# A fused attention and gated-layer kernel: first loads split over two queues, first projections k by k, and early copies shared by two engines

## Chip, cores and metric

One core of a Trainium2 chip. The metric is the device time of one execution in microseconds (us), median of several. A profile of one execution gives its span (first to last recorded instruction), what every engine did in it, and what each instruction waited for. PE is the tensor engine, PEld its weight loads, DVE the vector engine, ACT the scalar engine, POOL the general-purpose engine, SP the engine that issues most transfers.

## The reference, cut

```python
x = A_x                                   # [1, 2048, 512] bf16
xn = _layernorm(x, axis=-1)
# A: 32 heads of 16, causal, window of 256, then wo [512, 512]
#    q, k, v = xn @ wqkv [512, 1536];  p = softmax(mask(q k / 4));  o = p v;  A = o @ wo
# B: h = (xn @ w_gate) * (xn @ w_up)      [2048, 1792];  B = h @ w_down
return x + A + B
```

## The kernel before

The kernel has no fixed loop order. A planner in the kernel's source walks through the work with estimated durations and landing times and emits each instruction where its estimate says it will be ready. The tokens are taken in four chunks of 512; chunk 0 is projected in four blocks of 128 rows, since nothing else can run yet. Only these parts matter here:

```python
MM = 0.2158                       # the planner's unit of PE time
PSUM_COPY = {"V": (0.605, 0.69), "A": (0.49, 0.60)}   # took, latency on DVE / ACT
HOLD = 0.1
...
# prologue: the loads, in this order
load(nc.sync, self.Wqkv[:, 0:2, 1024:1536], w["qkv"][:, 0:2, 1024:1536])    # Wv, 256 KB
load(nc.scalar, self.x[:, 0, :], xv[:, 0, :])                               # x0, 128 KB
load(nc.sync, self.Wqkv[:, 2:4, 1024:1536], w["qkv"][:, 2:4, 1024:1536])    # Wv, 256 KB
load(nc.scalar, self.x[:, 1, :], xv[:, 1, :])                               # x1, 128 KB
for t, lo in ((2, 512), (3, 0)):                                            # Wk, x2, Wq, x3
    load(nc.sync, self.Wqkv[:, :, lo:lo + 512], w["qkv"][:, :, lo:lo + 512])
    load(nc.sync, self.x[:, t, :], xv[:, t, :])
...
self.keep_busy(42, 0)             # filler matmuls until the first real one
...
# planner: which engine takes a copy, and when a transpose may go first
key = (at + (0.3 if e == "A" and len(o.on) > 1 else 0.0) + (self.HOLD if o.rank and now0 else 0.0), o.rank, t)
t -= 0.3 * (d.name.startswith("turn") and t <= now + 0.25)
...
def first_chunk(self):
    land = (3.4, 3.95, 7.7, 9.6)  # planned landings of x0 to x3
    wv, wk, wq = 5.9, 7.3, 9.3    # and of the weights
    ...                           # per block b: bn_stats, bn_aggr (DVE), sqrt (ACT),
                                  # reciprocal, apply (DVE), transpose (PE, "turn"), copy of it, then V, K, Q
    last = self.op("masks", {"V": (0.15, 0.2)}, [self.at_["ap", 1, 0]], ...)
    def project(i, lo, tok=tok):
        for c in range(4):
            self.matmuls(self.M[i][:, 128 * c:128 * c + 128],
                         [(self.Wqkv[:, k, lo + 128 * c:lo + 128 * c + 128], self.xnT[0][:, k, tok]) for k in range(4)])
```

The softmax here doesn't subtract the row's maximum and nothing guards it: scores larger than these inputs give would overflow.

## Time and profile before

| | before |
|---|---|
| time, median of 3 (lowest to highest) | 265.63 us (265.57 to 265.79) |
| span of the profiled execution | 263.98 us |
| first transpose of real data on PE | 5.53 us |
| first gate matmul (steady work begins) | 15.50 us |
| last matmul starts | 260.22 us |
| last matmul to the end of the span | 3.75 us |

The rows below the span cut the execution into a start, a middle (from the first gate matmul to the last matmul, 244.72 us) and a tail. The pieces are compared by start times of single matmuls, because modelled ends hide gaps of up to 0.2 us. The lines of the page, of the waits, of the stretches and of the chain are in the prediction. One more view, the timeline of DVE (start, duration, engine, line, operation, tiles; in brackets the idle time ahead and what ended it):

```profile
3.41 0.69 DVE L591 BATCH_NORM_STATS2 st<-x 128x6 f32<-128x512 bf16 x1 [1.47 <-DMA x<-in_A_x_dram]
...
4.60 0.43 DVE L591 BATCH_NORM_STATS2 st<-x 128x6 f32<-128x256 bf16 x1 [0.29 <-DMA x<-in_A_x_dram]
```

The first line is the statistics of x0, as soon as it landed; the second is the first half of x1's, which waits 0.29 us for its load and holds x0's reciprocal behind it.

### The profile page before, as it was taken

To read this page: it belongs to the slowest core of one execution; us is meant where nothing else is said; L and a number is where in the kernel's file an instruction comes from. 1 tells how busy PE (TensorE), PEld (TensorE's weight loads), DVE (VectorE), ACT (ScalarE), POOL (GpSimd) and SP (SyncE) were. 2 spreads that over 40 slices of the span, in tenths; PEclk is the share of its full clock that TensorE was granted. 3 is DMA by queue.
4 is the path that set the end of the run, shared out by engine and by line. 5 is a ranking of instruction groups with operands and counts; after the bars stand their busy time and mean duration, and the time that the engine had idled before them with its cause. 6 is when DMAs were issued, how large, how long until landed. Compare 5 with 4: busy or idle time off the path is not lost.

```text
span 264.0 us, 8009 instructions
## 1 busy us (share of the span) xinstructions
PE 259.4 (98%) x3456; PEld 131.9 (50%) x3456; DVE 190.6 (72%) x368; ACT 165.0 (63%) x122; POOL 119.7 (45%) x272
## 2 busy tenths in 40 slices
PE   8999999999999999999999999999999999999994
PEld 7974444554444354455534354546535353545462
DVE  4999886978996548777997467786946268786504
ACT  3457576768776766687776767677777676572000
POOL 1406655475175635427084736437081828255000
PEclk9999999999999999999999999999999999999999
DMA  6999910000002200000005200000000100000002
GB/s 219 381 374 350 215 22 1 2 0 2 4 2 59 64 22 22 0 2 2 2 0 83 62 22 0 4 2 0 2 2 22 40 4 22 2 0 2 0 2 81
DMA packets 17251, 13.88 MB, mean 53 GB/s; under 512 B 7104, under 2 KB 17216, under 8 KB 17216
## 3 DMA queue, kind: packets, MB, share of 16 engines
q1 hardware_dynamic: 16784, 13.05, 18.0%
q8 instruction: 27, 0.44, 0.7%
q10 hardware_dynamic: 432, 0.33, 0.4%
q14 instruction: 8, 0.07, 0.1%
HBM read 9.70 MB, written 2.10 MB: 45 GB/s over the span
## 4 chain that ended last, share of the span: by engine, by line
PE 96%; DMA 2%; DVE 1%; ACTq 0%; issue 0%
PE M L207 72%; PE S L215 9%; PE M L245 7%; PE M L689 6%; DMA x<-in_A_x_dram 1%; DMA out_dram<-xn 1%; PE M L624 1%; PE S L207 1%; DVE xn L783 1%; DVE st L591 0%; ACTq L149 0%; DVE xn L273 0%; PE M L197 0%; DVE rs L603 0%
## 5 line engine op out<-in xcount | busy, mean ns | idle before, releaser
L498 ACT ACTIVATE P<-S 128x2048 bf16<-128x2048 f32 x76 | 140.9, 1854 | 57.1 <-PE S L215 50.5
L224 POOL TENSOR_SCALAR_AFFINE_SELECT P<-P 64x256 bf16<-64x256 bf16 (+1 forms) x248 | 112.6, 456 | 112.9 <-ACT P L498 100.7
L207 PE MATMUL M<-xnT,Wg 128*128 128x512 bf16 x224 | 57.7, 380 | 0.0
L207 PE MATMUL M<-xnT,Wu 128*128 128x512 bf16 x224 | 57.7, 380 | 0.0
L207 PE MATMUL M<-Wd,hT 128*128 128x512 bf16 (+1 forms) x224 | 51.8, 373 | 0.0
L741 DVE TENSOR_TENSOR hT<-M,gsb 128x512 bf16<-128x512 f32 x56 | 38.0, 678 | 8.4 <-PE M L207 8.1
L207 PEld LDWEIGHTS <-hT 128*128 128x128 bf16 x238 | 21.7, 98 | 23.4 <-issue 2.1
L207 PEld LDWEIGHTS <-Wu 128*128 128x128 bf16 x224 | 20.5, 98 | 24.8 <-issue 1.8
L207 PEld LDWEIGHTS <-Wg 128*128 128x128 bf16 x224 | 20.2, 98 | 24.3 <-issue 2.4
L203 DVE CAST gsb<-M 128x512 bf16<-128x512 f32 x41 | 28.1, 686 | 5.3 <-PE M L207 4.9
L207 PE MATMUL M<-xnT,Wqkv 128*128 128x128 bf16 (+1 forms) x224 | 30.3, 288 | 0.0
L215 PE MATMUL S<-Q,K 32*128 32x320 bf16 (+3 forms) x720 | 30.0, 254 | 0.0
L534 DVE STREAM_TRANSPOSE at<-M 128x512 f32<-128x512 f32 x32 | 21.3, 698 | 9.7 <-PE M L245 9.6
L215 PEld LDWEIGHTS <-K 32*128 32x128 bf16 x720 | 11.9, 92 | 31.8 <-issue 30.9
L230 DVE TENSOR_TENSOR P<-P,masks 128x512 int16<-128x512 int16 x56 | 22.6, 410 | 7.1 <-ACT P L498 7.1
L207 PEld LDWEIGHTS <-Wqkv 128*128 128x128 bf16 x224 | 15.9, 98 | 10.6 <-issue 1.5
L783 DVE TENSOR_TENSOR y<-M,x 128x512 bf16<-128x512 f32 x12 | 8.2, 687 | 16.5 <-PE M L207 16.3
L245 PE MATMUL M<-P,V 64*17 64x320 bf16 (+4 forms) x1440 | 19.5, 252 | 0.0
L245 PEld LDWEIGHTS <-V 64*17 64x17 bf16 x1440 | 17.1, 86 | 3.2 <-issue 1.3
L284 DVE TENSOR_SCALAR K<-M,own 128x512 bf16<-128x512 f32 x24 | 17.1, 743 | 2.1 <-PE M L207 2.1
L207 PE MATMUL M<-Wo,OT 128*128 128x512 bf16 (+1 forms) x64 | 16.6, 374 | 0.0
L689 PE MATMUL M<-Wqkv,xnT 128*64 128x256 bf16 x256 | 15.5, 274 | 0.0
(51 smaller groups left out, 138.0 us busy)
## 6 DMA issues: line engine op xcount, KB each, us to landing
Wg<-in_B_w_gate_dram SPq DMA_DIRECT2D x2, 896.0 KB, 10.2
Wu<-in_B_w_up_dram SPq DMA_DIRECT2D x2, 896.0 KB, 11.9
out_dram<-y SPq DMA_DIRECT2D x12, 128.0 KB, 1.7
Wqkv<-in_A_wqkv_dram SPq DMA_DIRECT2D x2, 512.0 KB, 6.1
x<-in_A_x_dram SPq DMA_DIRECT2D x1, 1024.0 KB, 13.6
Wd<-in_B_w_down_dram SPq DMA_DIRECT2D x2, 512.0 KB, 11.6
Wd<-in_B_w_down_dram SPq DMA_DIRECT2D x2, 384.0 KB, 8.7
Wqkv<-in_A_wqkv_dram SPq DMA_DIRECT2D x2, 256.0 KB, 3.5
```

What stands on the lines that cost most here:

```text
L203: self.nc.vector.tensor_copy(out=out, in_=in_)
L207: self.nc.tensor.matmul(ps, lhsT=a, rhs=b, start=first and n == 0, stop=last and n == len(pairs) - 1)
L215: self.nc.tensor.matmul(self.S[:, e, 64 * at:64 * (at + m)], lhsT=self.K[U % 3][rows, c, j].rearrange("p l t -> p (l t)"), rhs=self.Q[T % ...
L224: self.nc.gpsimd.affine_select(out=v, in_=v, pattern=[[0, 4], [0, n], [sign, 64]], base=0, fill=0.0, compare_op=ALU.is_gt if kind else ALU ...
L230: self.nc.vector.tensor_tensor(out=v, in0=v, in1=m, op=ALU.bitwise_and)
L245: self.nc.tensor.matmul(banks[lane][32 * e:32 * e + 17, 64 * q:64 * (q + m)], lhsT=self.V[U % 3][rows, j, 4 * c + e, 0:17], rhs=P[rows, e, ...
L284: self.nc.vector.tensor_scalar(out=out, in0=in_, scalar1=own, scalar2=None, op0=ALU.mult)
L498: ex = self.op(f"exp{g}", {"A": (took + 0.06, took + 0.18)}, [o], lambda e: self.nc.scalar.activation(out=P[:, :, 0:hi], in_=self.S[:, :, ...
L534: t = self.op(f"tr{v}", {"V": (0.63, 0.71)}, [o] + ts, lambda e, par=par: nc.vector.transpose(out=self.at[:, :, par, :], in_=self.M[banks[ ...
L689: self.nc.tensor.matmul(self.M[i][64 * lane:64 * lane + 64, 256 * jj:256 * jj + 256], lhsT=self.xnT[T % 2][:, k, tok], rhs=w[:, lane], sta ...
L741: x = self.op(f"u{T}.{f}", {"V": PSUM_COPY["V"]}, [o, ("gate", T, f)], lambda e: self.nc.vector.tensor_tensor(out=self.hT[T % 2][:, f, :], ...
L783: self.nc.vector.tensor_tensor(out=keep["y"][:, cols], in0=self.M[i][:, cols], in1=self.x[:, t, cols], op=ALU.add)
```

## The change

The intent: bring x1 early enough that DVE does not wait for it, bring Wv and Wk in pieces over both issuing queues, let a projection begin with the k pieces that are there (k numbers the four slices of 128 rows of a weight, which are summed up), spread the first chunk's copies over ACT and DVE alike, and build the masks when nothing needs DVE. The planner's estimates are renewed to match.

```diff
+KEYS_COPY = {"V": (0.68, 0.76), "A": (0.63, 0.70)}
-    HOLD = 0.1
+    HOLD = 0.2
@@ prologue
-        load(nc.sync, self.Wqkv[:, 0:2, 1024:1536], w["qkv"][:, 0:2, 1024:1536])
+        qkv(nc.sync, 1024, 0, 1)
         load(nc.scalar, self.x[:, 0, :], xv[:, 0, :])
-        load(nc.sync, self.Wqkv[:, 2:4, 1024:1536], w["qkv"][:, 2:4, 1024:1536])
-        load(nc.scalar, self.x[:, 1, :], xv[:, 1, :])
-        for t, lo in ((2, 512), (3, 0)):
-            load(nc.sync, self.Wqkv[:, :, lo:lo + 512], w["qkv"][:, :, lo:lo + 512])
-            load(nc.sync, self.x[:, t, :], xv[:, t, :])
+        load(nc.sync, self.x[:, 1, :], xv[:, 1, :])
+        qkv(nc.scalar, 1024, 2, 4)
+        qkv(nc.sync, 1024, 1, 2)
+        qkv(nc.scalar, 512, 2, 4)
+        qkv(nc.sync, 512, 0, 2)
+        load(nc.sync, self.x[:, 2, :], xv[:, 2, :])
+        qkv(nc.sync, 0, 0, 4)
+        load(nc.sync, self.x[:, 3, :], xv[:, 3, :])
-        for f, g in ((0, 4), (4, 8), (8, 11), (11, 14)):
+        for f, g in ((0, 7), (7, 14)):
             load(nc.sync, self.Wd[:, f:g], w["d"][:, f:g])
@@ run, loop, choose
-        self.now, self.mode = 5.4, "D"
-        self.free = {"V": 3.0, "A": 4.5, "G": 3.0, "S": 6.0}
+        self.now, self.mode = 4.8, "D"
+        self.free = {"V": 3.0, "A": 3.4, "G": 3.0, "S": 6.0}
-  key = (at + (0.3 if e == "A" and len(o.on) > 1 else 0.0) + ...
+  key = (at + (0.3 if e == "A" and len(o.on) > 1 and not now0 else 0.0) + ...
-  t -= 0.3 * (d.name.startswith("turn") and t <= now + 0.25)
+  t -= 0.5 * (d.name.startswith("turn") and t <= now + 0.4)
@@ first_chunk
-        land = (3.4, 3.95, 7.7, 9.6)
-        wv, wk, wq = 5.9, 7.3, 9.3
+        land = (3.45, 3.9, 7.2, 9.6)
+        wv, wk, wq = 5.4, 6.6, 9.2
-        last = self.op("masks", {"V": (0.15, 0.2)}, [self.at_["ap", 1, 0]], ...
+        last = self.op("masks", {"V": (0.15, 0.2)}, [self.at_["ap", 3, 0]], ...
-                for c in range(4):
-                    self.matmuls(self.M[i][:, 128 * c:128 * c + 128],
-                                 [(self.Wqkv[:, k, lo + 128 * c:lo + 128 * c + 128], self.xnT[0][:, k, tok]) for k in range(4)])
+                for k in range(4):
+                    for c in range(4):
+                        self.nc.tensor.matmul(
+                            self.M[i][:, 128 * c:128 * c + 128], lhsT=self.Wqkv[:, k, lo + 128 * c:lo + 128 * c + 128],
+                            rhs=self.xnT[0][:, k, tok], start=k + c == 0, stop=k == 3, skip_group_check=True)
  ... (copies of K planned with KEYS_COPY; transposes, V, K and Q of chunk 0 planned shorter) ...
```

More of the change, by code (lines that the diff above doesn't have):

```diff
@@ L149, in load, with qkv @@
             eng.dma_start(out=dst, in_=src)
-        load(nc.sync, self.Wqkv[:, 0:2, 1024:1536], w["qkv"][:, 0:2, 1024:1536])
+        def qkv(eng, lo, k0, k1):
+            load(eng, self.Wqkv[:, k0:k1, lo:lo + 512], w["qkv"][:, k0:k1, lo:lo + 512])
+        qkv(nc.sync, 1024, 0, 1)
         load(nc.scalar, self.x[:, 0, :], xv[:, 0, :])
-        load(nc.sync, self.Wqkv[:, 2:4, 1024:1536], w["qkv"][:, 2:4, 1024:1536])
-        load(nc.scalar, self.x[:, 1, :], xv[:, 1, :])
-        for t, lo in ((2, 512), (3, 0)):
-            load(nc.sync, self.Wqkv[:, :, lo:lo + 512], w["qkv"][:, :, lo:lo + 512])
-            load(nc.sync, self.x[:, t, :], xv[:, t, :])
+        load(nc.sync, self.x[:, 1, :], xv[:, 1, :])
[6 more added lines that the diff above has]
+        load(nc.sync, self.x[:, 3, :], xv[:, 3, :])
         h = self.F // 2
@@ L338, in loop @@
                     at = max(t, self.free[e])
-                    key = (at + (0.3 if e == "A" and len(o.on) > 1 else 0.0) + (self.HOLD if o.rank and now0 else 0.0), o.rank, t)
+                    key = (at + (0.3 if e == "A" and len(o.on) > 1 and not now0 else 0.0) + (self.HOLD if o.rank and now0 else 0.0), o.rank, t)
                     if best is None or key < best[0]:
@@ L611, in first_chunk @@
             out=self.warm[:], in_=self.warm[:], func=ACT.Exp), rank=1)
-        last = self.op("masks", {"V": (0.15, 0.2)}, [self.at_["ap", 1, 0]], lambda e: nc.vector.memset(self.masks[:], -1), rank=9)
+        last = self.op("masks", {"V": (0.15, 0.2)}, [self.at_["ap", 3, 0]], lambda e: nc.vector.memset(self.masks[:], -1), rank=9)
         for n in range(5):
@@ L643, in k_out @@
                 for lane in range(2):
-                    x = self.op(f"K0b{b}", PSUM_COPY, [o, x], lambda e, lane=lane: self.i_keys(
+                    x = self.op(f"K0b{b}", KEYS_COPY, [o, x], lambda e, lane=lane: self.i_keys(
                         e, 0, slice(0, 4), lane, self.M[i].rearrange("p (c t) -> p c t", c=4), slice(2 * b, 2 * b + 2)), rank=1)
@@ L658, in first_chunk @@
             for n, ks in enumerate(([0, 1], [2, 3]) if b == 0 else ([0, 1, 2, 3],)):
-                self.A.insert(at + n, Dense(f"turn{b}", 1.3 * len(ks) / 4, [("ap", b, n)], lambda i, f=turn, ks=ks: f(i, ks),
+                self.A.insert(at + n, Dense(f"turn{b}", 1.1 * len(ks) / 4, [("ap", b, n)], lambda i, f=turn, ks=ks: f(i, ks),
                                             lambda o, i, f=turned, ks=ks: f(o, i, ks)))
             self.add_v(0, b, wv)
-            self.add(f"k0b{b}", 4.85, [("xnT", 0, b), wk], lambda i, f=project: f(i, 512), k_out)
-            self.add(f"q0b{b}", 4.85, [("xnT", 0, b), wq], lambda i, f=project: f(i, 0), q_out)
+            self.add(f"k0b{b}", 4.4, [("xnT", 0, b), wk], lambda i, f=project: f(i, 512), k_out)
+            self.add(f"q0b{b}", 4.4, [("xnT", 0, b), wq], lambda i, f=project: f(i, 0), q_out)
     def norms(self, T):
@@ L699, in add_v @@
         x = [("xnT", T, b)] if T + b else [("xnT", 0, 0, 0), ("begun", 0, 0, 2)]
-        self.add(f"v{T}.{b}", 4 if T else 4.4, x + [land] + self.ring(T, 2)[:1 if T == 3 else 0], emit, evac, "C")
+        self.add(f"v{T}.{b}", 4, x + [land] + self.ring(T, 2)[:1 if T == 3 else 0], emit, evac, "C")
     def add_qk(self, T, c):
@@ L708, in k_out @@
             for lane in range(2):
-                x = self.op(f"K{T}.{c}", PSUM_COPY, [o, x], lambda e, lane=lane: self.i_keys(
+                x = self.op(f"K{T}.{c}", KEYS_COPY, [o, x], lambda e, lane=lane: self.i_keys(
                     e, T, slice(c, c + 1), lane, self.M[i].unsqueeze(1)), rank=1)
```

## The prediction

> **What bounds the kernel now.** I read the page first (busy shares), then the waits of PE, then the stretch table, then the chain of waits and the timeline of the first 16 us. One core, so no dies to compare; its granted clock is 1.00.
>
> ```profile
> span 264.0 us, 8009 instructions
> PE 259.4 (98%) x3456; PEld 131.9 (50%) x3456; DVE 190.6 (72%) x368; ACT 165.0 (63%) x122; POOL 119.7 (45%) x272
> ```
>
> PE is the only engine near its limit. Its waits over the whole span, as the trace attributes them, are two:
>
> ```profile
> PE M L197 <- PEq L817: 0.8, 1, 0.8
> PE M L624 <- DVE xn L273: 0.2, 1, 0.2
> ```
>
> The first is the launch, the second the wait for the first normalised rows. The stretch table (columns: us, then busy us and count of PE, PEld, DVE, ACT, POOL, clock, DMA share, GB/s) confirms it:
>
> ```profile
> 5.50:10.50 5.00, 4.92 (x76) 4.20 (x76) 4.43 (x14) 1.60 (x5) 2.31 (x10) 1.00 1.04 364
> 10.50:15.50 5.00, 4.97 (x89) 4.92 (x89) 4.87 (x12) 4.15 (x8) 0.70 (x3) 1.00 1.07 374
> 20.50:240.00 219.50, 219.50 (x2985) 103.73 (x2982) 165.15 (x310) 155.02 (x105) 113.51 (x248) 1.00 0.13 30
> 240.00:264.00 24.00, 20.50 (x203) 11.27 (x201) 9.06 (x15) 0.00 (x0) 1.32 (x3) 1.00 0.07 24
> ```
>
> The reader is to see that from 5.5 us on PE has no visible idle time until about 260.5 us; after that come 3.5 us of last additions and stores. The change touches the loads, the first chunk and the costs by which the kernel's own planner orders work. So only the time before steady work, and the little that PE loses between 5.5 and 17 us, is there to win. The chain of waits from the start of the span (start, us, what) shows the first part:
>
> ```profile
> 1.25 3.33 DMA x<-in_A_x_dram
> ...
> 4.60 0.43 DVE st L591
> 5.03 0.07 DVE rs L603
> 5.10 0.03 issue
> 5.13 0.36 DVE xn L273
> 5.49 0.05 issue
> 5.53 0.54 PE M L624 x4
> 6.08 0.23 PE M L197 x4
> 6.31 1.05 PE M L689 x16
> 7.36 0.04 issue
> 7.40 0.40 PE M L624 x4
> 7.79 2.75 PE M L207 x48
> 10.55 0.03 issue
> 10.58 0.40 PE M L624 x4
> ```
>
> The first real matmul (the transpose, L624) stands behind the load of x1, not of x0. x0's statistics end at 4.32 and its square root (ACT, 4.35 for 0.29) at 4.64. But DVE's program puts half of x1's statistics before x0's reciprocal. That half waits idle from 4.32 to 4.60 for x1, which landed at 4.58. So reciprocal and apply start about 0.28 us late, and so does the transpose. The filler matmuls (L197) end by then:
>
> ```profile
> 0.84 4.47 PE L197 MATMUL M<-const-bfloat16-1.0 128*128 128x128 bf16 x42 [0.84 <-PEq L817]
> 5.53 0.54 PE L624 MATMUL M<-ident,xn 128*128 128x128 bf16 x4 [0.22 <-DVE xn L273]
> ```
>
> PE's busy time hides more. A matmul's modelled end lies some 0.2 us after its last issue, so I also took start-to-start times of single matmuls. The hidden gaps after 5.1 us are 0.38 (filler to transpose), 0.14 (between the halves of the first transpose), 0.15 (filler to the V projection), 0.21 (V projection to the second transpose) and 0.19 (before the third transpose, whose input ends at 10.11 + 0.41 = 10.52): 1.07 us in all. Nothing else in the first chunk exceeds 0.1. The rest, about 16 us over 174 places, is some 0.1 us at each change between kinds of matmul (score, value, dense), spread over the whole run.
>
> **What the Trainium skill says.**
> - "TensorE: Matmul & The Clock Gate", section "Wait — 56ns, not 53.3ns?": warm matmuls of 128 columns follow each other at 55.6 ns. The trace agrees: 48 projections take 2.75 us in the chain, 57 ns each. So the projections already run at the pipeline's pace.
> - "DMA: Bandwidth & Descriptors", section "Issuing engines are not separate DMA queues": transfers from SP and ACT share the same 16 engines; another issuer saves only issue time. The trace has 0.43 to 0.50 us per issue on SP and 350 to 381 GB/s in the loaded slices. Two queues cannot load faster; they can only change what lands first.
> - "PSUM — Partial Sum Buffer", section "The four PSUM rules": the start flag clears the written-bits of a whole bank, so four interleaved sums in one bank need it on the first matmul only. The new loop does exactly this (start only at k = c = 0), so I expect right results; no run here shows it yet.
> - "ScalarE: Activation LUTs", section "What ACT_TABLE_LOAD costs": about 1283 ns per table load. The trace has 1.28 us, twice (1.74 and 13.64). The number of switches stays.
>
> **The change, part by part.**
>
> 1. Loads. Before x2, the same 256 KB of x, 512 KB of Wv and 512 KB of Wk are moved in both kernels. x1 goes from second on ACT, beside two 256 KB pieces of Wv, to second on SP behind one 128 KB piece. Between 4.02 and 5.11 us x1 and the second Wv piece (384 KB) landed, 357 GB/s. With x0 and the first piece landed near 3.4, x1 and an equal share of ACT's Wv piece are 256 KB, so 0.73 us: x1 at about 4.1 (estimate), before DVE asks at 4.32. DVE's idle 0.28 us goes, and the transpose can start at 5.53 - 0.28 = 5.25; the 42 fillers, unchanged, were last issued at 5.10. Gain 0.25. ACT issues one more load (0.45 us), so its first table load ends near 3.5 and its warm-up by 3.7, before the first root at 4.35: free.
>
> 2. Wk in halves on both queues. It landed at 7.54; the plan now counts on 6.6. The bytes ahead are the same. If it comes before the V projection ends (about 6.85), K of the first rows can fill the 0.21 us gap; otherwise the second transpose comes first, as now. The planner also allows a longer wait for a transpose (preference 0.5 instead of 0.3), so the gap may simply remain. I book 0.05 to 0.1.
>
> 3. k by k. The same 8 x 16 matmuls at 57 ns: no saving in work. 4.4 instead of 4.85 is only the planner's estimate (in units of 0.2158 us, 0.95 instead of 1.05; measured 0.91). The order lets a projection start with the pieces that are there, but Wv and Wk are needed late enough. Zero.
>
> 4. Copies on ACT and DVE alike until the first scores. In 10.5 to 15.5 DVE is busy 4.87 of 5 us; ACT has 4.15, but only 1.60 in the five before and an idle stretch of 2.64 us just before the first exp at 17.77. Moving copies to ACT takes load from DVE. PE had dense work in the meantime, so the gain is what PE waited: the 0.19 before the third transpose, of which I book 0.15. The first scores may move from 17.33 to about 16.5, but that pays nothing by itself: the same PE work follows, and exp has slack (ACT is 63% busy and does nothing after 240).
>
> 5. Masks later. One memset of 0.33 us leaves DVE at 7.35, where it delays a copy of V and a transposed copy. POOL's ten selects (2.86 us) start near 12.5 instead of 7.75 and end near 15.5, long before the first select at 19.72. PE was fed, so about 0.05, inside the item above.
>
> 6. Wd in two loads, not four: SP's issues are blocked there anyway and the data are needed much later. Zero.
>
> Sum: 0.25 + 0.1 + 0.15 + about 0.1 from the small gaps around the first transpose = 0.6 us. 265.63 - 0.6 = 265.0.
>
> **The rivals.**
> - Lost in replanning. New cost figures shift the first scores and with them the static order of about 76 score batches and 16 value groups. One score batch more or fewer that stands alone between dense work costs or saves two changes, about 0.19 us (6.7 us over 70 entries and 5.3 over 58 exits). Three either way is 0.55 us, as large as the gain. For: the plan is sensitive. Against: PE had no wait at all after 24 us, so the order had slack. It gives 264.5 to 265.6.
> - A load takes the place of the wait. Wv in three pieces on two queues could land later than the V projection asks, or the smaller pieces make x0 later than 3.39. For: Wk took 2.4 us after Wv for 512 KB, slower than the rest. Against: Wv had landed at 5.11 and is asked for at 6.05. If x0 slips 0.2 and Wk is late, 265.4 to 265.9.
> - ACT becomes the slow link. With no handicap, copies queue there in front of the roots that gate the transposes, and in front of the 1.28 us table load, so scores come later. For: an ACT copy takes 0.60 to 0.63 us. Against: ACT is idle for most of the first 10 us, and roots outrank copies. 265.3 to 266.
> - Everything works: all 1.07 us of gaps go, 264.5, and with a lucky replanning 264.2.
>
> **Range and chances.** The gain is bounded above by about 1.1 us of early gaps plus about 0.5 of planning luck, and a loss by a few waits of some tenths. Predicted 265.0, range 264.2 to 265.8. Two per cent is 5.3 us, five times the gaps available: faster 0.01, within 2% 0.98, slower 0.01.
>
> **What would show it.** Step 1: x1 landing before 4.32, no DVE idle before the second statistics, the first transpose at 5.25 to 5.35. Steps 2 and 4: gaps before the second and third transposes under 0.1, Wk landed before 7, K and V copies in ACT's rows before 13 us. Step 3: 48 projections still at 57 ns. Replanning: PE without waits after 24 us, and the number of changes of kind near 174. It would be wrong if PE shows a wait over 0.5 us after 6 us, if x1 still lands after 4.5, or if the last matmul moves by more than the first one did: then the middle, not the start, decided.

## The result, and the profile after

| | before | after |
|---|---|---|
| time, median (lowest to highest, runs) | 265.63 us (265.52 to 265.79, 6) | 265.56 us (265.37 to 265.97, 6) |
| ratio after / before, 95% interval | | 0.9999 (0.9986 to 1.0012) |
| span of the profiled execution | 263.98 | 263.72 |
| first transpose | 5.53 | 5.59 |
| first gate matmul | 15.50 | 15.46 |
| middle | 244.72 | 244.95 |
| tail | 3.75 | 3.31 |

A ratio is the mean time of one kernel's runs over the mean of the other's in the same rounds, so it is not quite the ratio of the medians quoted. The result is "the same": an interval of about 0.13% either way (0.35 us) covers both zero and a good part of the 0.6 us that was predicted. The single times do not settle a few tenths; start times inside a profile do. The page after:

```profile
span 263.7 us, 8001 instructions
PE 259.5 (98%) x3456; PEld 131.9 (50%) x3456; DVE 187.7 (71%) x363; ACT 167.7 (64%) x127; POOL 119.7 (45%) x272
```

Five instructions went from DVE to ACT, as meant (368 to 363, 122 to 127). The waits of PE, of which before had two:

```profile
PE M L204 <- PEq L826: 0.8, 1, 0.8
```

The wait for the first normalised rows is gone from this list because the fillers stayed slow for longer (by the timeline they end at 0.84 + 4.64 = 5.48, before at 5.31) and cover most of it; the transpose itself starts 0.06 us later. The stretch table (busy us and count of PE, PEld, DVE, ACT, POOL, then clock, DMA share, GB/s):

```profile
5.50:10.50 5.00, 4.77 (x76) 4.17 (x77) 3.75 (x12) 3.56 (x9) 0.00 (x0) 1.00 1.02 357
10.50:15.50 5.00, 5.00 (x93) 5.00 (x91) 3.79 (x10) 4.24 (x7) 2.16 (x10) 1.00 1.06 376
20.50:240.00 219.50, 219.44 (x2984) 103.56 (x2977) 164.26 (x309) 153.34 (x105) 112.01 (x244) 1.00 0.14 31
240.00:264.00 24.00, 20.68 (x204) 11.33 (x202) 9.28 (x15) 1.35 (x1) 2.90 (x7) 1.00 0.07 24
```

Between 5.5 and 15.5 us DVE is busy 3.75 + 3.79 = 7.5 us instead of 9.3, and ACT 7.8 instead of 5.8. PE was fed before and is fed now: its 9.8 us of busy time did not grow. The chain of waits from the start (start, us, what):

```profile
0.80 2.89 DMA x<-in_A_x_dram
...
3.72 0.70 DVE st L598
...
5.59 0.41 PE M L631 x2
...
7.57 0.40 PE M L631 x4
7.96 1.79 PE M L646 x32
9.76 0.27 PE M L631 x4
10.03 2.68 PE M L646 x48
```

The first link was the load of x1 and is now that of x0, which landed at 3.70; before, its statistics could start at 3.41. The DVE timeline after says the same:

```profile
3.72 0.69 DVE L598 BATCH_NORM_STATS2 st<-x 128x6 f32<-128x512 bf16 x1 [1.78 <-DMA x<-in_A_x_dram]
...
4.55 0.40 DVE L598 BATCH_NORM_STATS2 st<-x 128x6 f32<-128x256 bf16 x1
```

DVE no longer idles before x1's statistics, since x1 landed at 4.22, but everything begins 0.31 us later. Note also in the chain that the third transpose (9.76 by this view, 9.63 by the record of its first matmul) now stands after two projections and not after three.

Summed up, the start gained 0.04, the middle lost 0.23, the tail gained 0.44: 0.26 us of span. The time fell by 0.07, less than the span. So there are four questions: why the start gained nothing, what the middle lost, why the tail became shorter, and where the rest of the span's gain went.

### The profile page after: what moved, and what is told of

Read it like the earlier page. It is cut to its first block, busy times and chain, and to the rows that moved or that the text cites. A ratio compares the mean times of both kernels' runs of the same rounds, so it can differ in the third digit from the quotient of the medians.

```text
span 263.7 us, 8001 instructions
## 1 busy us (share of the span) xinstructions
PE 259.5 (98%) x3456; PEld 131.9 (50%) x3456; DVE 187.7 (71%) x363; ACT 167.7 (64%) x127; POOL 119.7 (45%) x272
## 4 chain that ended last, share of the span: by engine, by line
PE 95%; DMA 2%; DVE 1%; ACT 1%; issue 0%; ACTq 0%
PE M L214 69%; PE S L222 9%; PE M L252 7%; PE M L698 6%; PE M L646 3%; DMA x<-in_A_x_dram 1%; ACT P L505 1%; DMA out_dram<-xn 1%; PE S L214 1%; DVE xn L792 1%; PE M L631 0%; DVE st L598 0%; ACT xnT L208 0%; DVE xn L280 0%; ACT ve L607 0%
## 5 line engine op out<-in xcount | busy, mean ns | idle before, releaser
L214 PE MATMUL M<-xnT,Wqkv 128*128 128x512 bf16 x96 | 23.0, 380 | 0.0
L291 DVE TENSOR_SCALAR K<-M,own 128x512 bf16<-128x512 f32 x21 | 15.1, 742 | 2.7 <-PE M L214 1.9
L698 PE MATMUL M<-Wqkv,xnT 128*64 128x256 bf16 x256 | 15.5, 274 | 0.1
L698 PEld LDWEIGHTS <-xnT 128*64 128x64 bf16 x256 | 13.4, 110 | 2.0 <-issue 1.6
```

Of the source, the lines that this page charges most:

```text
L214: self.nc.tensor.matmul(ps, lhsT=a, rhs=b, start=first and n == 0, stop=last and n == len(pairs) - 1)
L291: self.nc.vector.tensor_scalar(out=out, in0=in_, scalar1=own, scalar2=None, op0=ALU.mult)
L698: self.nc.tensor.matmul(self.M[i][64 * lane:64 * lane + 64, 256 * jj:256 * jj + 256], lhsT=self.xnT[T % 2][:, k, tok], rhs=w[:, lane], sta ...
```

## The experiments

The first theory after reading the two traces: the loads move x0 later as much as they move x1 earlier, the rest of the change moves copies that nothing waited for, and the tail and the middle are changed by something that is in neither part of the intent. The rival: each part gains what it was meant to, and the other loses it again.

All twelve runs gave right results. For each, "turn0" is the start of the first transpose. "Ratio" is against the kernel before in the same rounds.

| run | turn0 | first gate matmul | middle | tail | span | median us (runs) | ratio (95%) |
|---|---|---|---|---|---|---|---|
| before | 5.53 | 15.50 | 244.72 | 3.75 | 263.98 | 265.63 (6) | |
| after | 5.59 | 15.46 | 244.95 | 3.31 | 263.72 | 265.56 (6) | 0.9999 (0.9986 to 1.0012) |
| before_again | 5.27 | 16.06 | 244.71 | 3.69 | 264.47 | 265.92 (4) | 1.0007 (0.9994 to 1.0020) |
| after_again | 5.61 | 15.50 | 244.95 | 3.28 | 263.73 | 265.73 (6) | 1.0005 (0.9993 to 1.0017) |
| loads_only | 5.51 | 15.58 | 244.87 | 3.74 | 264.19 | 265.85 (5) | 1.0003 (0.9991 to 1.0015) |
| rest_only | 5.27 | 16.05 | 244.82 | 3.28 | 264.15 | 265.49 (5) | 0.9993 (0.9981 to 1.0005) |
| before_dve1 | 5.56 | 15.53 | 244.72 | 3.69 | 263.94 | 265.49 (6) | 0.9987 (0.9973 to 1.0002) |
| after_dve8 | 5.59 | 15.71 | 244.94 | 3.57 | 264.22 | 266.04 (6) | 1.0006 (0.9991 to 1.0020) |
| after_act1 | 5.52 | 15.69 | 244.82 | 3.29 | 263.80 | 265.71 (6) | 0.9998 (0.9981 to 1.0015) |
| x_split | 5.27 | 15.93 | 244.98 | 3.29 | 264.20 | 266.65 (6) | 1.0037 (1.0018 to 1.0057) |
| before_tail | 6.16 | 17.38 | 244.71 | 3.26 | 265.35 | 265.79 (6) | 1.0010 (0.9985 to 1.0036) |
| x2_late | 5.61 | 15.30 | 244.82 | 3.34 | 263.46 | 265.46 (6) | 0.9991 (0.9977 to 1.0005) |
| c_by_c | 5.54 | 15.45 | 244.95 | 3.33 | 263.73 | 265.50 (4) | 0.9987 (0.9968 to 1.0005) |
| x0_head | 5.30 | 15.94 | 244.82 | 3.85 | 264.61 | 266.58 (6) | 1.0029 (1.0014 to 1.0044) |

Most intervals include 1, so nearly every verdict below rests on start times inside one profile per kernel. That profile can be an unusual execution: those of before_again and rest_only are the slowest of their kernels (spans 264.5 and 264.2 us, the others 264.0 to 264.4 and 263.4 to 263.6), that of x_split is the fastest. The middle repeats to 0.01 us between profiles of one plan, the tail to 0.06. The start does not, as the first run shows.

### before_again: the kernel before, once more

No edit.

> The kernel before, unchanged, for the scatter. Theory 1 (the new load order makes x0 land later, which eats the 0.28 us won from x1): x0 lands at 3.35 to 3.45 again, x1 near 4.6, first transpose at 5.5 to 5.6. Theory 2 (the 0.31 us by which x0 came later in the changed kernel is chance of one profile): x0's landing differs from 3.39 by 0.2 us or more. Both: time ratio 1.000 within 0.001.

Measured: the first transpose came 0.26 us earlier than in the first profile, because x1 happened to land at 4.32 instead of 4.58. That is the very gain the change was made for, and yet the first gate matmul came 0.56 us *later*. The timeline of PE tells why:

```profile
8.15 3.00 PE L207 MATMUL M<-xnT,Wqkv 128*128 128x128 bf16 x48 [0.61 <-DMA Wqkv<-in_A_wqkv_dram]
```

PE stood 0.61 us before the first K projection, for Wk, which landed at 8.10 here and at 7.54 in the first profile. From matmul number 128, counted from 0 (11.149 against 11.709), to the last one the two executions stay 0.554 to 0.560 us apart. So nothing in 250 us gives a delay back: PE has no slack, and a tenth won or lost before 15 us is a tenth at the end. This makes start times a fair measure, and it shows that the same binary varies by as much as the predicted gain.

### after_again: the changed kernel, once more

No edit.

> The changed kernel, unchanged. Theory 1: x0 lands at 3.6 to 3.8 again, first transpose at 5.5 to 5.65; the PE wait of 0.22 us near 208 us is there again because it belongs to the order of instructions. Theory 2: x0 lands at 3.4 to 3.5 this time, first transpose at 5.25 to 5.35 and a time 0.2 to 0.3 us below before. Time by theory 1: 265.4 to 265.7.

Measured: turn0, first gate matmul, middle and tail repeat the first profile to 0.04 us. Wk's later half landed at 7.3 to 7.6 in all seven profiles with the new order of loads, against 6.65 to 8.10 for Wk in five with the old. So Wk's landing is steadier in the profiles of the new order; whether the halves or the order do that was not tested apart, and the times are no steadier for it (265.55 to 266.54 here, 265.47 to 266.16 for the kernel before in the same rounds). Its first gate matmuls (15.45 to 15.71, and 15.30 in x2_late) are no earlier than those of the two better profiles of the kernel before with the old order (15.50, 15.53) unless the plan is mended too.

### loads_only: the new loads in the kernel before

```diff
 # before, with the load block of the change (the ten small loads, Wd in two)
```

> The kernel before with the new load orders alone (the Wd loads too); planner figures, copies, k by k and masks as before. Theory 1: x0 at 3.6 to 3.8, x1 at 4.2 to 4.3, first transpose within 0.1 of 5.55, gap before the third transpose still there or smaller because x2 comes earlier, no wait at 208; time within 0.2 of before. Theory 2: first transpose near 5.3 and 0.25 us less time.

Measured: turn0 5.51 and first gate matmul 15.58, within 0.13 of both kernels. The loads alone make neither a gain nor a loss. Landings over all profiles, by order of loads:

| landing, us | old order (5 profiles) | new order (7 profiles) |
|---|---|---|
| x0 | 3.30 to 3.48 | 3.57 to 3.71 |
| x1 | 4.30 to 5.21 | 4.13 to 4.56 |
| Wk, last piece | 6.65 to 8.10 | 7.26 to 7.56 |
| x2 | 7.22 to 8.56 | 7.67 to 7.93 |
| first packet on SP's queue | 2.13 to 2.39 | 1.82 to 1.83 |
| first packet on ACT's queue (x0) | 1.85 to 1.86 | 1.95 to 2.01 |

x0 is the same 128 KB on the same queue in both. With a first piece of 128 KB instead of 256 KB on SP, SP's packets start 0.3 to 0.6 us sooner, before x0's, and by the end of x0's packets SP's queue had moved 170 to 232 KB instead of 77 to 133. x0 lands later with the new order on each of three chips, so the chip is not the reason. The order of the two first packets is measured; that it is the cause of x0's 0.2 to 0.3 us is tested by the last experiment.

The middle is 0.15 us longer than before's with the same plan: see the section on after_act1.

### rest_only: the changed kernel with the old loads

```diff
 # after, with the load block of the kernel before
```

> The changed kernel with the load orders of before (Wd too). Theory 1: x0 near 3.39, x1 near 4.58, first transpose at 5.53 as before; the third transpose no longer waits (0.19 us won), the wait near 208 us remains (0.22 lost): time within 0.15 of before, and the trace about level with the changed kernel's. Theory 2 (loads carry a gain, the new order loses it): time 0.2 to 0.3 us above before.

Measured: turn0 5.27 (x1 landed early, at 4.30) but first gate matmul 16.05 (Wk at 7.94), the same pair as in before_again. Middle 244.82 and tail 3.28. The third transpose waited 0.46 us, against the expectation, since x2 landed only at 8.27. The late start is that of one execution: the other four have spans 0.6 to 0.8 us shorter, and if their middle and tail are those of this profile, their first gate matmul came at 15.3 to 15.5 (estimate from their spans, known to 0.1 us). So the old loads cost the new plan nothing that shows. The tail's 0.4 us belongs to the rest of the change and not to the loads. The middle of the new plan, 244.82, is 0.10 us longer than that of the old one. That is all that the replanning costs: counted over the hidden gaps at changes of kind after 16.5 us, 174 of 16.21 us in total before, 175 of 16.32 us here.

### before_dve1: one more DVE instruction in the kernel before

```diff
         nc.vector.memset(self.eps[:], 1e-5)
+        nc.vector.memset(self.eps[:], 1e-5)
```

Why such an odd edit: each engine's program closes with an instruction DRAIN and some waits. The views leave these out; their times here are from the trace's records. In the trace of before, DVE's closing drain comes 0.39 us behind SP's, and in that of after 0.03 us. Counting the records of DVE from 0, waits and drains included, the late drain is number 447 = 63 + 3 x 128. Shifting the count by one should take the delay away, if the count is what matters.

> The kernel before with one more tiny memset on DVE at the start, where DVE idles. Theory 3 (the end of the span depends on which instruction of DVE's own program is number 447 counted from 0, that is 63 + 3 x 128: in the kernel before it is the drain of the closing barrier, which comes 0.38 us after the other engines' drains): the drain is now number 448, DVE's drain comes within 0.1 us of the others, the stretch from the last matmul's start to the end of the span falls from 3.7 to 3.3 us, time 0.3 to 0.45 us lower. Theory 4 (the shorter tail of the changed kernel comes from its order of stores): the tail stays at 3.7 us, time unchanged.

Measured: DVE's drain came 0.03 us after SP's, so the delay left it. But the tail fell by 0.06 only, because POOL's second closing drain, number 324 of POOL's records, still came 0.32 us after the clearing of semaphores before it. In after it is number 318 and comes after 0.03 us. (POOL's 324 does not leave the same remainder as 447; only that it moves with the count is shown.) Two engines were late side by side; removing one shows the other. The median fell by 0.32 us against the kernel before beside it, as much as theory 3 had asked for, although the tail, its reason, hardly moved: times of this scatter can't judge here.

### after_dve8: eight more DVE instructions in the changed kernel

```diff
         nc.vector.memset(self.eps[:], 1e-5)
+        nc.vector.memset(self.eps[:], 1e-5)     # eight times
```

> The changed kernel with eight more tiny memsets on DVE at the start, so that its closing drain becomes number 447. Theory 3: the drain comes 0.38 us after the others, the tail grows from 3.3 to 3.7 us, time 0.3 to 0.45 us above the changed kernel, so 266.0 to 266.2. Theory 4: tail stays 3.3 us.

Measured: DVE has 449 records again, as in before; its drain is late by 0.41 us and the tail grows from 3.28 to 3.31 (two profiles) to 3.57. This is the reverse of before_dve1, and together with before_tail below they show that the tail depends on how many instructions an engine's program has, not on what they do. The change shortened the tail by accident: DVE has 441 records instead of 449 and POOL 321 instead of 327.

This run shows also that the third transpose can wait:

```profile
9.90 0.40 PE L639 MATMUL M<-ident,xn 128*128 128x128 bf16 x4 [0.25 <-DVE xn L288]
```

It follows x2's landing (7.93) by 1.96 us. In after x2 landed at 7.67 and the transpose started at 9.63, 1.96 us later too; so it is, to 0.01 us, in all six profiles of this plan.

### after_act1: one more ACT instruction in the changed kernel

```diff
         self.warm = warm
+        nc.scalar.activation(out=warm[:], in_=warm[:], func=ACT.Sqrt)
```

The middle of after is 0.23 us longer than before's, of which rest_only explained 0.10. In the trace one exp of after starts 0.34 us after the end of its wait (206.90 after 206.56), where the median of all such pairs is 0.045 (in before, too). By count it is number 191 of ACT's records, 63 + 128; number 63 of after, an exp behind a wait as well, is late by 0.36. In before neither number is an exp. The timeline around it, of after:

```profile
206.11 0.40 PE L222 MATMUL S<-Q,K 32*128 32x320 bf16 x8
206.90 1.88 ACT L505 ACTIVATE P<-S 128x2048 bf16<-128x2048 f32 x1 [1.00 <-PE S L222]
208.83 0.40 PE L222 MATMUL S<-Q,K 32*128 32x256 bf16 x8
```

The next scores on PE wait for this exp to free their bank; PE loses 0.22 us before 208.83.

> The changed kernel with one more 128x1 activation at ACT's start, in idle time. Theory 3: the exp at 206.9 us, ACT's instruction number 191 (63 + 128), started 0.34 us after its wait ended and held PE's next scores 0.22 us; now number 191 is the wait ahead of it, which stands in idle time, so PE's 0.22 us gap near 208 us goes, the exp follows its wait within 0.05 us, and the last matmul starts 0.2 us earlier relative to the 128th one. Theory 5 (the gap comes from the new order of work itself, a wait for a buffer): the gap stays. Time 265.3 to 265.5 by theory 3.

Measured, the same place with ACT's count shifted by one:

```profile
206.34 0.40 PE L223 MATMUL S<-Q,K 32*128 32x320 bf16 x8
206.84 1.88 ACT L506 ACTIVATE P<-S 128x2048 bf16<-128x2048 f32 x1 [0.70 <-PE S L223]
208.94 0.40 PE L223 MATMUL S<-Q,K 32*128 32x256 bf16 x8
```

The exp starts 0.50 us after the first of its scores instead of 0.79, and PE's gap is gone. The middle is 244.82, as in rest_only, which has 225 ACT records and whose number 191 is no exp behind a wait. So 0.13 of the 0.23 us is one late exp. PE's gap was 0.22, so 0.09 of it was made up or is lost elsewhere. loads_only shows the same: its 220 ACT records put exps behind waits at numbers 63 and 191 (late by 0.36 and 0.32), PE stands 0.24 us after the second, and its middle is 0.15 over before's.

What lies behind the count is suggested, not shown. The page lists eight transfers of a kind "instruction" of 8192 bytes on the queue q14; some of them fall near the late instructions (207.6 in after, 212.2 in loads_only, 262.3 in before). 8192 bytes over 128 records is 64 bytes each. The Trainium skill, "Runtime: NRT & Kernel Launch", section "Instruction fetch mechanics", says that each engine's instruction memory is a first-in-first-out store refilled in blocks of 16 KiB, 256 instructions, and that crossing a block is "mostly hidden". PE's 27 transfers of 16 KB for 6,925 records (27.05 x 256) agree with that. If the transfers on q14 are those of the other engines, their blocks have half that size, and the crossing is not hidden where an instruction there stands directly behind a wait: 0.3 to 0.4 us.

### x_split: x0 and x1 in halves of 64 rows on both queues

```diff
-        qkv(nc.sync, 1024, 0, 1)
-        load(nc.scalar, self.x[:, 0, :], xv[:, 0, :])
-        load(nc.sync, self.x[:, 1, :], xv[:, 1, :])
+        for t in (0, 1):
+            load(nc.sync, self.x[0:64, t, :], xv[0:64, t, :])
+            load(nc.scalar, self.x[64:128, t, :], xv[64:128, t, :])
         qkv(nc.scalar, 1024, 2, 4)
-        qkv(nc.sync, 1024, 1, 2)
-        qkv(nc.scalar, 512, 2, 4)
-        qkv(nc.sync, 512, 0, 2)
+        qkv(nc.sync, 1024, 0, 2)
+        qkv(nc.sync, 512, 0, 4)
-        self.keep_busy(42, 0)
+        self.keep_busy(35, 0)
 # and the planner's landing times and start moved accordingly
```

> The changed kernel with x0 and x1 first, each in two halves of 64 rows on SP and ACT, then Wv in two halves, Wk whole; 35 fillers instead of 42 and the planner told so. Theory 1 (in the new order x0's packets share the engines with Wv's first piece from the start, so x0 comes 0.3 us later than before): x0 lands at 2.8 to 3.1, first transpose at 4.7 to 5.0 instead of 5.6. But K's first projection then waits for Wk (landing 7.2 to 8.0), so of 0.7 us only 0.0 to 0.4 remain at the 128th matmul. Theory 2 (x0's landing is chance): x0 at 3.4 to 3.7.

Measured: x0's halves landed at 3.01 and 3.23, the earliest of all. But ACT's three issues took 0.58, 0.87 and 0.61 us, so its table load began only at 2.96 and the root of x0 at 4.36; the first transpose came at 5.27, no earlier than rest_only's. V then stood 0.26 us and K 0.44 us for weights that landed later (Wk at 7.95). First gate matmul 15.93. The kernel is slower by 0.37%: what was sent first landed first, and what it displaced was waited for. SP's first transfer here, 64 KB over 64 rows, sent its first packet only at 2.16 us, so a small first piece is not always an early one. Its profiled execution was the fastest of its six (266.13; the others 266.37 to 267.38), so its full loss is not in the profile. With only 35 fillers a late warm-up of the tensor engine's clock is suspected there (see before_tail), not shown.

### before_tail: one more DVE and four more POOL instructions in the kernel before

```diff
+        nc.gpsimd.memset(self.mhalf[:], -0.5)   # four more
         nc.vector.memset(self.eps[:], 1e-5)
+        nc.vector.memset(self.eps[:], 1e-5)
```

> The kernel before with one more tiny memset on DVE and four more on POOL at the start, in idle time. The run with the DVE memset alone moved DVE's closing drain (from 0.39 to 0.03 us behind SP's) but not the tail, because POOL's second closing drain was as late. Theory 3, widened to POOL (its instruction number 324 is late in the kernel before; in the changed kernel number 324 is never reached): now both come at once, the tail from the last matmul to the end of the span falls from 3.7 to 3.3 us, time about 265.2 to 265.4, ratio 0.998 to 0.999. If POOL's delay is no matter of position, the tail stays at 3.7 us.

Measured: with both counts shifted, the tail is 3.26 instead of 3.75, as short as that of the changed kernel. The shorter tail can be had in the old kernel by adding five useless instructions. The times cannot show it: they run from 265.20 (the lowest single time of any run here) to 267.33. The profiled execution (267.06) shows one reason for such scatter. The stretch of the V projection:

```profile
7.00:9.00 2.00, 2.00 (x19) 1.25 (x16) 0.90 (x3) 0.43 (x2) 0.46 (x2) 1.00 1.07 365
```

The clock column says 1.00, but in the records V's pairs of matmuls follow each other at 212 to 213 ns, where before's take 106, and projections of 128 columns at 106 instead of 56 ns until about 10 us. The fillers, too, had stayed at 107 ns to their end, while they fell to 58 ns at about 3.7 us in before_again and at 5.04 in before. The engine was at half pace for the first 10 us, and the first gate matmul came at 17.38. The Trainium skill, "TensorE: Matmul & The Clock Gate", section "Part 1: The HAM clock gate (the "warmup" mystery)", says that the clock passes half or all pulses and that the warm-up point varies from run to run with a free-running window. The halves of the pace and the variation agree. The delay here, 9 us after the first filler, is longer than the 3.4 us that it gives for the window; but it speaks of sustained activity, and PE stood still for 0.68 us before the transpose at 6.16. Whether that is why full pace came so late is not shown.

### x2_late: the planner told that x2 lands late

```diff
-        land = (3.45, 3.9, 7.2, 9.6)
+        land = (3.45, 3.9, 7.9, 9.6)
```

The change lowered the planned landing of x2 from 7.7 to 7.2, and so its plan puts the third transpose after two projections. x2 really lands at 7.67 to 7.93 with these loads.

> The changed kernel with one number of the planner changed: x2's landing 7.9 instead of 7.2 us (four profiles had 7.67 to 7.93), so that the third transpose stands after three projections instead of two. Theory 6 (in the changed kernel the third transpose stands too early for x2, and PE waits 0.04 to 0.46 us for it depending on the landing): the gap before the third transpose is below 0.08 whatever x2's landing, the first gate matmul starts at 15.3 to 15.5 instead of 15.46 to 15.71. Rival (PE waits there for DVE or ACT work, not for x2): the gap stays at 0.1 or more. Time 265.2 to 265.6; the later order of work is replanned and may add or take 0.2.

Measured:

```profile
7.71 2.84 PE L646 MATMUL M<-xnT,Wqkv 128*128 128x128 bf16 x48
10.39 0.39 PE L631 MATMUL M<-ident,xn 128*128 128x128 bf16 x4
10.61 1.95 PE L646 MATMUL M<-xnT,Wqkv 128*128 128x128 bf16 x32
```

Three projections run first, the transpose follows without a wait, and the first gate matmul comes at 15.30, the earliest of all profiles. (Of the 0.20 us to after_again, 0.18 are this wait. Of the 0.16 us to after only 0.04 are; 0.10 are a longer gap before V there.) The number 191 of ACT is no exp here either, so the middle is 244.82. The span, 263.46, is the shortest of all. In time this best candidate is 0.9991 (0.9977 to 1.0005) of the kernel before: lower, but not told apart from it.

### c_by_c: the old order of the projection's loop

```diff
-                for k in range(4):
-                    for c in range(4):
-                        ...
+                for c in range(4):
+                    self.matmuls(self.M[i][:, 128 * c:128 * c + 128], [...])
```

> The changed kernel with the projections of the first chunk written as before, column block by column block. All theories: the same 57 ns per matmul (48 in 2.84 us with the last one's tail), because Wk is there in both halves before K starts; no difference in the first gate matmul beyond the landing's scatter (15.4 to 15.75), time 265.4 to 265.8. If k by k mattered, the projections start later or run slower here by 0.1 us or more.

Measured: first gate matmul 15.45 against 15.46 and 15.50 with k by k, the middle the same to 0.01, single projections 55.8 to 55.9 ns apart in both. Working k by k is worth nothing here. Both kernels give right results, so a single start flag per bank for four interleaved sums is right.

### x0_head: the first piece on SP made 256 KB again

```diff
-        qkv(nc.sync, 1024, 0, 1)
+        qkv(nc.sync, 1024, 0, 2)
         load(nc.scalar, self.x[:, 0, :], xv[:, 0, :])
-        load(nc.sync, self.x[:, 1, :], xv[:, 1, :])
+        load(nc.scalar, self.x[:, 1, :], xv[:, 1, :])
         qkv(nc.scalar, 1024, 2, 4)
-        qkv(nc.sync, 1024, 1, 2)
-        qkv(nc.scalar, 512, 2, 4)
-        qkv(nc.sync, 512, 0, 2)
+        qkv(nc.sync, 512, 0, 4)
 # on x2_late
```

> The changed kernel with x2's planned landing at 7.9 (as in the run before) and another order of loads: SP begins with a 256 KB piece of Wv and then Wk whole, ACT has x0, x1 and the second piece of Wv. Theory 1 (x0 lands 0.15 to 0.4 us earlier when SP's first transfer is the 256 KB piece, whose packets start at 2.1 to 2.4 us instead of 1.83): x0 at 3.3 to 3.5 as in the five profiles with the old order (3.30 to 3.48), not 3.57 to 3.71 as in the seven with the new one; x1 at 4.3 to 4.7; first transpose at 5.25 to 5.6; Wk at 7.1 to 7.8; first gate matmul at 15.2 to 15.4 if Wk comes before 7.5, later one for one if not; mid part 244.82, tail 3.3, span 263.3 to 263.7. If SP's first piece is not the cause, x0 lands at 3.6 to 3.7. Time 265.1 to 265.6.

Measured: x0 landed at 3.28 and the first transpose started at 5.30. So what delayed x0 was what SP sends first. The run undid two things at once, the small first piece and x1's place right behind it on SP, and does not tell them apart. But Wv's second piece, now third on ACT's queue, landed at 7.46:

```profile
6.17 0.63 PE L696 MATMUL M<-Wqkv,xnT 128*64 128x256 bf16 x8
7.50 0.63 PE L696 MATMUL M<-Wqkv,xnT 128*64 128x256 bf16 x8 [0.71 <-DMA Wqkv<-in_A_wqkv_dram]
```

The V projection stands still in its middle (0.98 us from the start of its 8th matmul to that of its 9th, where 0.11 is the pace: 0.87 lost), and the kernel is 0.29% slower. Its tail of 3.85 us has a hole of 0.47 us in SP's closing waits (263.20 to 263.67) with nothing landing in it; that stays unexplained.

### Time outside the span

Every execution has both a time and a span (the latter kept to 0.1 us). Their difference, averaged over each kernel's runs, falls into two groups:

| kernels | time less span, us |
|---|---|
| before (11 runs in each of four batches), before_again, loads_only, before_dve1, before_tail | 1.69 to 1.73 |
| after, after_again, rest_only, after_dve8, after_act1, x_split, x2_late, c_by_c, x0_head | 1.90 to 1.95 |

All kernels with the new plan have 0.2 us more outside what is recorded, with either order of loads and with any tail. The profiled pair has 265.68 - 263.98 = 1.70 and 265.53 - 263.72 = 1.81. The records of instructions end with the last closing waits. Those of transfers run on, and they part the kernels in the same way: in all nine profiles of the second group a transfer of the kind "instruction" with 8192 bytes starts on q14 1.72 to 1.75 us after the end of the span; in the five of the first group none starts later than 0.58 us after it. Which engine it is for, the records do not say. The lengths of two engines' programs go with the groups too (ACT 219 or 220 records against 224 to 227; POOL 327 or 331 against 321). POOL's number 324, late in before, lies just beyond the last record of the second group, so its delay may have moved out of the span and not gone. This is a lead and no proof. No run was made for it; this stays open.

## Why the prediction was right or wrong

The time was right: 265.56 lies in the range of 264.2 to 265.8, and "within 2%" came out. The sum behind it was not. It put 0.6 us on the way from 265.63 to 265.0. The start gained 0.04 in the profiled pair, and what else moved came from places that the prediction did not have.

1. **Loads (0.25 booked, about 0 measured).** The step that failed is "With x0 and the first piece landed near 3.4". It took x0's landing from the trace of before as given and let only x1 move. x1 landed at 4.22, near the 4.1 predicted (4.13 to 4.30 in six of the seven profiles of the new order), and DVE's idle time before its statistics went. But x0 landed 0.2 to 0.3 us later (loads_only, x0_head), which put the transpose at 5.59 instead of 5.25 to 5.35. This was the first half of the second rival ("the smaller pieces make x0 later than 3.39"). The premise that an earlier transpose is an earlier end failed as well: before_again, rest_only, x_split and x0_head have it at 5.27 to 5.30 and reach the first gate matmul at 15.93 to 16.06, later than all that have it at 5.5 to 5.6 (15.30 to 15.71). In x_split and x0_head the loads that brought x forward put a weight back; in the other two, the slowest executions of their kernels, the early x met a late Wk.
2. **Wk in halves (0.05 to 0.1 booked).** Wk did not come before 7: it landed at 7.26. K's first projection moved from 7.63 to 7.6 to 7.8 and follows the second transpose, whose 0.21 us gap stays. What came with the new order is a narrower scatter of Wk's landing, for which one profile of before could give no number.
3. **k by k (zero).** Right, by c_by_c.
4. **Copies on both engines (0.15 booked).** DVE's load fell by 1.8 us in the first chunk and ACT took it, as said. The third transpose's wait fell from 0.19 to 0.04 in after, but in the other profiles of that plan it is 0.18 to 0.46, since the transpose now waits for x2 and not for DVE. The planner's new landing time for x2 did this, not the copies; x2_late shows the cause, with a first gate matmul 0.15 to 0.20 us earlier than in after, after_again and c_by_c. The side remark that the first scores would come at 16.5 was wrong too: 17.28 after 17.33.
5. **Masks, and 6. Wd in two loads (zero).** Nothing in the runs speaks against it: POOL's selects start after 10.5 and PE had no wait on either.
7. **Replanning (a rival, 0.55 either way).** It is far smaller: 0.10 us, one change of kind more. The other 0.13 of the middle is one exp at an unlucky place in ACT's program; in the old kernel no exp stands at such a place.
8. **The tail (not in the prediction).** "After that come 3.5 us of last additions and stores" was taken as fixed. It became 0.44 us shorter because the counts of DVE's and POOL's instructions changed; five added instructions do the same for the old kernel (before_tail).
9. **Time outside the span (not in the prediction).** 0.2 us of the shorter span came back there.

In sum over the pair: -0.04 (start) + 0.23 (middle) - 0.44 (tail) = -0.25, the -0.26 of the spans with rounding. About 0.1 (the pair) to 0.2 (the means) of that is given back outside the span, which leaves some -0.1; the medians differ by -0.07, and the interval is wider than either (0.35 us each way). So the time lies in the range by the width of the range and by luck, not by the mechanism: of the parts booked only the third transpose's 0.15 came, in one profile of its plan, and the middle and the tail were not booked. One of the prediction's own signs of being wrong came true: the last matmul moved by more than the first transpose (0.18 us against 0.06), so the middle decided and not the start. No run found the predicted 0.6: the best start, x2_late's 15.30, is 0.20 earlier than 15.50. The gaps of 1.07 us are real, but those before V (0.15) and before the second transpose (0.20) stand in most profiles with either order of loads, and the bytes that must land before 8 us are the same.

## What to carry to other kernels

When the bytes ahead of the first work are fixed, an order of loads that brings one operand forward puts another back: add up the landings of all that the first stage needs, from several profiles, before booking the gain of one. Profile the old kernel twice or more before judging tenths at the start; here the same binary differed by 0.56 us with nothing changed. Split the span at fixed matmuls into start, middle and tail, and compare time less span too, since parts that have nothing to do with the change can move as much as the parts that have.

## What the Trainium skill lacked or had wrong

- "Runtime: NRT & Kernel Launch", section "Instruction fetch mechanics": the crossing of a block is not always hidden. Records number 63 and 191 of ACT, 447 of DVE and 324 of POOL came 0.3 to 0.4 us late where they stood directly behind a wait (POOL's behind a clearing of semaphores); shifting the count took it away (middle -0.13 us with ACT shifted, tail from 3.75 to 3.26 us with DVE and POOL both shifted). Transfers of 8192 bytes on these engines' queue, not 16 KiB, go with it. The cause is inferred.
- "DMA: Bandwidth & Descriptors", section "Issuing engines are not separate DMA queues": it says only that another issuer saves issue time. Not said is how much one queue's first transfers delay the other's: with 128 KB of Wv and then x1 first on SP instead of 256 KB of Wv, its first packet came at 1.82 to 1.83 us instead of 2.13 to 2.39, and the x0 of the other queue at 3.57 to 3.71 us instead of 3.30 to 3.48. Size alone does not set the first packet: 64 KB over 64 rows sent it at 2.16 us (x_split).
- "TensorE: Matmul & The Clock Gate", section "Part 1: The HAM clock gate (the "warmup" mystery)": it puts the change to full pace around 4 us into sustained matmul activity, give or take 0.5 us. Here the fillers reached it between 2.8 us (before_again) and 4.2 us (before) after the first of them in six profiles, and not before their end in the other eight. In before_tail half pace lasted until about 10 us (212 to 213 ns between matmuls of 256 columns, 106 when warm), with PE idle for 0.68 us in between, while the profile's clock figure stood at 1.00.
- No page has the scatter of landings: the same loads brought Wk in at 6.65 to 8.10 us in five profiles.
- No page has the part of the time outside the span that depends on the program: 1.69 to 1.73 us for one plan and 1.90 to 1.95 us for the other.
